# Relu of q on ScalarE from the fifth pair on, indicator rows of head 1 copied by VectorE, loads of pair 0 on one queue, and a new order

## The chip, the cores and the metric

The kernel runs on one core of a Trainium2 chip. A core has five engines, each of which works through its own list of instructions in order: PE (TensorE, matmuls and transposes), DVE (VectorE), ACT (ScalarE), POOL (GpSimd) and SP (SyncE, which here only issues DMAs). They meet at semaphores. DMAs move data between HBM and the on-chip memory SBUF, spread over 16 DMA engines. PE writes its results to PSUM, from where DVE and ACT read them; POOL reads SBUF alone.

The metric is the device time of one execution in microseconds (us).

## The reference

Two parts follow one another. The first is an attention with selected chunks, for 4 batches of 8 heads, 768 positions and 64 dimensions per head:

```
k_min, k_max = min and max of k over each chunk of 32 keys          # 24 chunks
ub     = sum_d max(q*k_min, q*k_max)                                # a bound per query and chunk
ub     = where(chunk of query >= chunk, ub, -1e9)
top    = the 6 chunks with the largest ub
mask   = (chunk of key in top) and (query >= key)
attn   = softmax(where(mask, q k^T / 8, -1e9))
x      = attn v, heads side by side                                 # 4 x 768 x 512
```

The second is a gated MLP on x, per batch:

```
h      = gelu(x w_in);  u, v = the two halves of h                  # 1024 -> 512 + 512
v_s    = w_sg (normalised v * g_ln) + b_sg                          # mixes the 768 positions
out    = x + (u * v_s) w_out
```

## The kernel before

*Pairs and windows.* The 32 heads are worked in 16 pairs (two heads share the 128 partitions). Buffers of a pair are reused: four windows (w = p % 4) of keys KA, queries QA and values vx, three sets of loaded rows (qn, kn, vn), three of transposed queries qT and of their relu rT.

*What happens to a pair* (`prep`, L1003). `kside` (L539): two DMAs bring the heads' rows of k; PE transposes them (L534), DVE takes minimum and maximum of each chunk of 32 (L562) into W, ACT evacuates the transposed k into KA (L439); DVE subtracts, so that W holds the minimum and the difference (L581). `qside` (L584): the same transposes for q, evacuated to qT by ACT (or by DVE for two pairs); then relu of columns 192 to 767 of qT into rT, a VectorE tensor_scalar with max 0 (L600); then POOL casts qT to bf16 into QA (L606). The bound is q times the minimum plus relu(q) times the difference, so the small matmuls `ub` (L641 for single pairs 0 to 3, L688 for pairs taken in twos from 4 on) need qT, rT and W of all their pairs. DVE transposes the bounds (L651, L697), finds the sixth largest of each row (`max`, L658, L708), compares (L664, L713) and transposes the result to Dt (L668, L716): one where a chunk isn't selected. Only columns from 192 on take part, since the first 192 queries have at most six chunks.

*How the mask reaches the scores.* For pairs 0 to 3 (`scores`, L772) extra matmuls (L804) add an indicator of the chunks times Dt to q k^T. From pair 4 on (`scores_full`, L736) each head has a window of its own, KA[w][0] and KA[w][1] of 128 rows: 64 rows of keys and 64 of the indicator INDF; the queries' window QA has Dt in the matching rows, brought by four DMAs from Dt on SP for each two pairs (L721). One matmul of 128 rows then gives the masked score (L757). ACT takes the exponential (L763, L813), POOL zeroes the part above the diagonal (L768, L820), PE multiplies by v (L836, L843), DVE divides (L851, L853).

*The indicator rows.* `mask_rows` (L725) runs when a window goes over from the first kind to the second, for windows 0 to 3. For both heads i it copies the 64 rows of INDF into KA[w][i], by a DMA on SP (L730), and has POOL clear the rows of QA (L733). For i = 0 the copy overwrites rows 64 to 127 of KA[w][0], in which the keys of the second head stood until then: it has to wait for the scores of pair w, and ACT's evacuation of k for pair w + 4 waits for it. Pairs 8 to 15 have their rows restored by another DMA (L578), after a DMA from KA to KA (L575).

*Loads.* Each load of q, k or v is one DMA per head on SP (L517, L526); for pair 0 alone the second head's loads of k and q go out from ACT's queue (`BOTH = 1`, used in L517). The weights follow on SP too.

*The MLP* (`moe_h` L871, `moe_g` L930) starts for each batch when its four pairs are done: transposes of x (L865, evacuated by ACT at L439), v half (L881, gelu L886), statistics (L891, L893) and normalising (L909) on DVE, u half (L920, gelu L926), the mixing (L938) with two DVE instructions per product (L955, L959), the last product (L971) and the residual (L980), then the store (L987).

*What sets the order.* The program is first written down as 1338 operations in the natural order (`P.op`, each with its engine, reads and writes). `TABLE` (L1057) then gives, for each engine, the order in which it issues them by their numbers, the PSUM slot of each tile and the places of some filler matmuls that keep PE busy at the start (L374). `Program.place` and `link` (L100, L122) take dependencies from the reads and writes, whatever the order, and turn them into semaphore waits. An engine waits at the head of its list: what is behind a waiting instruction waits too. That holds for the DMAs on SP as well.

Of the kernel before, what the change touches and what calls it, by code (L numbers as in the profile page):

```python
# [260 lines left out]
def _build(nc, ctx, q, k, v, w_in, g_ln, w_sg, b_sg, w_out, out):  # L261
    B, H, S, DH = q.shape
# [50 lines left out]
    BOTH = 1  # L313
    KBIG = 16
    VHACT = ()
    RELP = ()
    DNP = ()
# [266 lines left out]
    def qside(p):  # L584
# [14 lines left out]
        for x, (a, z) in enumerate(((LO, TG), (TG, S)) if p < RELH else ((LO, S),)):  # L599
            P.op("pool" if p in RELP else "dve", lambda d, a=a, z=z: d.tensor_scalar(  # L600
                rT[r][:, a - LO:z - LO], qT[r][:, a:z], 0.0, None, op0=ALU.max),
                gps(z - a, 60) if p in RELP else dve(z - a, rate=2), ("rel", p), port=True,
                reads=[qk[x]] if p < RELH else qk, writes=[("rT", r, x)] if p < RELH else [("rT", r, 0), ("rT", r, 1)])
# [121 lines left out]
    def mask_rows(w):  # L725

        for i in range(2):
            m0 = 64 * (1 - i)
            if i == 1 or (w if w >= HALF else w + NW) < KSPR:
                P.op("sp", lambda e, i=i, m0=m0: e.dma_start(KA[w][i][m0:m0 + 64, :], INDF[m0:m0 + 64, :]),  # L730
                     dmac(590), ("mrow", w, i, 0), reads=["INDF"], dma=f"mrow{i}", xfer=450,
                     writes=[("KI", w, i)] + ([("KA", w, 0, 0), ("KA", w, 0, 1)] if i == 0 else []))
# [303 lines left out]
    for p in range(4, NP + 4):  # L1036
# [39 lines left out]
    "act": (  # L1076
# [11 lines left out]
    "dve": (  # L1088
# [18 lines left out]
    "pool": (  # L1107
# [81 lines left out]
```

## Time and profile before

| | us |
|---|---|
| median of 3 runs | 221.12 (220.24 to 221.32) |
| the profiled execution | 221.28 |
| its span, from the first to the last instruction | 219.2 |
| PE busy in the span | 206.2 (94%) |
| DVE busy | 188.5 (86%) |
| ACT busy | 161.4 (74%) |
| POOL busy | 89.2 (41%) |

The profile names each group by line, engine, operation, and out<-in by the program's names, then the count, the busy time, the mean duration in ns, and the idle time of the engine just before, with what ended it. PEld is the loading of weights into PE, which overlaps PE's matmuls. Ends of matmuls are modelled, so PE busy is not PE at its peak. In lists of waits, "A <- B: total, times, longest" means that A's engine stood idle until B was done. SPq and ACTq are the engines' sequencers issuing DMAs. The chain of waits is followed back from the last instruction: at each step to what released it or to the instruction before it on its engine.

### The profile page before, as it was taken

To read this page: it belongs to the slowest core of one execution; us is meant where nothing else is said; L and a number is where in the kernel's file an instruction comes from. 1 tells how busy PE (TensorE), PEld (TensorE's weight loads), DVE (VectorE), ACT (ScalarE), POOL (GpSimd) and SP (SyncE) were. 2 spreads that over 40 slices of the span, in tenths; PEclk is the share of its full clock that TensorE was granted. 3 is DMA by queue.
4 is the path that set the end of the run, shared out by engine and by line. 5 is a ranking of instruction groups with operands and counts; after the bars stand their busy time and mean duration, and the time that the engine had idled before them with its cause. 6 is when DMAs were issued, how large, how long until landed. Compare 5 with 4: busy or idle time off the path is not lost.

```text
span 219.2 us, 6022 instructions
## 1 busy us (share of the span) xinstructions
PE 206.2 (94%) x2365; PEld 137.0 (63%) x2380; DVE 188.5 (86%) x542; ACT 161.4 (74%) x246; POOL 89.2 (41%) x119
## 2 busy tenths in 40 slices
PE   7969999899998999898999999999999999999994
PEld 3545768755756577686466676788745668545652
DVE  2899997879998999795999999998798776779894
ACT  3358989987469876799869787899986988764000
POOL 8415767973319445661323543663402141002000
PEclk9999999999999999999999999999999999999999
DMA  8999998993799998999999909433001002102107
GB/s 156 218 218 236 234 233 188 356 327 68 176 221 250 232 256 233 212 226 219 221 212 201 210 3 222 139 109 105 21 18 27 3 0 99 51 0 96 48 28 262
DMA packets 84651, 34.70 MB, mean 158 GB/s; under 512 B 77200, under 2 KB 79760, under 8 KB 84624
## 3 DMA queue, kind: packets, MB, share of 16 engines
q1 hardware_dynamic: 82768, 33.54, 63.8%
q10 hardware_dynamic: 1856, 0.79, 1.5%
q8 instruction: 19, 0.31, 0.7%
q14 instruction: 8, 0.07, 0.1%
HBM read 24.77 MB, written 6.29 MB: 142 GB/s over the span
## 4 chain that ended last, share of the span: by engine, by line
PE 61%; DVE 23%; ACT 7%; DMA 3%; SPq 3%; issue 2%; DVEq 0%; ACTq 0%
PE PSG L938 10%; PE PSC L757 9%; PE PSG L971 8%; PE PSG L534 6%; PE PSG L836 6%; PE PSG L920 5%; PE PSG L881 5%; DVE W L562 4%; ACT E L763 4%; DMA KA<-INDF 3%; PE PSG L688 3%; PE PSC L374 2%; PE PSG L843 2%; DVE stats L891 2%; PE PSC L798 2%; DVE PSG L955 2%
## 5 line engine op out<-in xcount | busy, mean ns | idle before, releaser
L763 ACT ACTIVATE E<-PSC 128x1024 bf16<-128x1024 f32 (+1 forms) x72 | 63.1, 924 | 6.4 <-PE PSC L757 5.8
L757 PE MATMUL PSC<-QA,KA 128*128 128x128 bf16 (+2 forms) x336 | 37.9, 246 | 1.1 <-ACT E L763 1.1
L562 DVE TENSOR_REDUCE W<-PSG 128x12 f32<-128x384 f32 x64 | 32.5, 545 | 4.5 <-PE PSG L534 4.4
L938 PE MATMUL PSG<-wsgT,vhat 128*128 128x384 bf16 x192 | 34.9, 326 | 0.8 <-DVE uT L959 0.4
L606 POOL CAST QA<-qT 64x768 bf16<-64x768 f32 (+1 forms) x28 | 24.2, 867 | 22.5 <-ACT qT L439 18.5
L768 POOL TENSOR_SCALAR_AFFINE_SELECT E<-E 128x768 bf16<-128x768 bf16 x24 | 20.8, 865 | 30.8 <-ACT E L763 30.4
L757 PEld LDWEIGHTS PSC<-QA,KA 128*128 128x128 bf16 x336 | 24.3, 98 | 10.3 <-ACT E L763 3.0
L926 ACT ACTIVATE uT<-PSG 128x384 bf16<-128x384 f32 x32 | 15.4, 492 | 16.6 <-PE PSG L920 16.0
L439 ACT ACTIVATE KA<-PSG 128x384 bf16<-128x384 f32 (+1 forms) x38 | 18.5, 493 | 10.1 <-DVE W L562 8.0
L938 PEld LDWEIGHTS PSG<-wsgT,vhat 128*128 128x128 bf16 x192 | 18.0, 98 | 12.1 <-DVE uT L959 0.9
L920 PE MATMUL PSG<-xT,winb 128*128 128x384 bf16 x128 | 24.1, 326 | 0.0
L813 ACT ACTIVATE E<-PSC 128x1024 bf16<-128x1024 f32 (+3 forms) x26 | 21.3, 858 | 3.6 <-PE PSC L804 3.4
L955 DVE SCALAR_TENSOR_TENSOR PSG<-PSG,glnT,bsgbc 128x384 f32<-128x384 f32 x32 | 19.7, 619 | 4.0 <-PE PSG L938 3.9
L881 PE MATMUL PSG<-winb,xT 128*128 128x512 bf16 x93 | 21.9, 379 | 0.2
L971 PE MATMUL PSG<-woutb,uT 128*128 128x512 bf16 (+1 forms) x88 | 21.1, 369 | 0.5
L836 PE MATMUL PSG<-vx,E 128*128 128x65 bf16 x480 | 19.6, 194 | 1.1 <-DVE XS L853 0.8
L836 PEld LDWEIGHTS PSG<-vx,E 128*128 128x128 bf16 x480 | 17.3, 98 | 2.8 <-DVE XS L853 1.1
L616 POOL CAST vx<-vn 128x768 bf16<-128x768 f32 x16 | 13.2, 828 | 13.7 <-DMA vn<-in_v_dram 7.7
L853 DVE TENSOR_TENSOR XS<-PSG,rden 128x384 bf16<-128x384 f32 x32 | 17.6, 554 | 0.8
L959 DVE TENSOR_TENSOR uT<-PSG,uT 128x384 bf16<-128x384 f32 x32 | 17.6, 554 | 0.8
L920 PEld LDWEIGHTS PSG<-xT,winb 128*128 128x128 bf16 x128 | 11.7, 98 | 9.8 <-ACT uT L926 1.4
L534 PE MATMUL PSG<-identF,kn 128*128 128x128 f32 x96 | 16.3, 288 | 1.4 <-ACT KA L439 0.8
(85 smaller groups left out, 345.6 us busy)
## 6 DMA issues: line engine op xcount, KB each, us to landing
vn<-in_v_dram SPq DMA_DIRECT2D x32, 192.0 KB, 4.1
kn<-in_k_dram SPq DMA_DIRECT2D x31, 192.0 KB, 4.5
qn<-in_q_dram SPq DMA_DIRECT2D x31, 192.0 KB, 4.5
out_dram<-osb SPq DMA_DIRECT2D x18, 256.0 KB, 2.8
uT<-in_moe_w_sg_dram SPq DMA_DIRECT2D x4, 384.0 KB, 6.5
KA<-INDF SPq DMA_DIRECT2D x16, 96.0 KB, 3.6
vgb<-in_moe_w_in_dram SPq DMA_DIRECT2D x3, 512.0 KB, 7.7
out_dram<-vgb SPq DMA_DIRECT2D x4, 256.0 KB, 2.0
```

The lines of the kernel that those rows point to most:

```text
L534: r = e.matmul(t.ap()[:, 128 * j:128 * j + 128], src[:, 3 * hf + j].rearrange("p i d -> p (i d)"), identF[:], is_transpose=True)
L562: P.op("dve", lambda d, m=m, op=op, src=src, h0=h0, h1=h1: d.tensor_reduce(W[w][:, m, 12 * h0:12 * h1].rearrange("p (h c) -> p h c", h=h1 ...
L606: P.op("pool", lambda g, i=i, r0=r0, r1=r1: g.tensor_copy(QA[w][i or 0][r0:r1, :], qT[r][r0:r1, :]), gps(S, 250 if i == 1 else 150), ("qca ...
L757: r = e.matmul(t.ap()[:, o:o + n], KA[w][i][:, 128 * kb:128 * kb + 128], QA[w][i][:, q0:q0 + n], start=True, stop=True)
L763: P.op("act", lambda e, t=t, c0=c0, c1=c1, i=i: e.activation(E[es][:, i, c0:c1], t.ap()[:, 0:c1 - c0], ACTF.Exp, scale=SCALE), act(c1 - c0 ...
L813: P.op("act", lambda e, t=t, c0=c0, c1=c1, n=n: e.activation(E[es][:, :, c0:c1], t.ap().rearrange("p (i x) -> p i x", i=2)[:, :, 0:n], ACT ...
L836: r = e.matmul(t.ap()[:, 65 * qb:65 * qb + 65], E[es][:, i, a:a + 128], vx[w][:, kb, i, :], start=first, stop=False, skip_group_check=True)
L881: r = e.matmul(t.ap()[:, 0:F], xT[s][:, dk, 128 * qt:128 * qt + 128], winb[:, dk, F:DFF], start=(dk == 0), stop=(dk == NDK - 1), skip_grou ...
L920: r = e.matmul(t.ap()[:, 0:TG], winb[:, dk, 128 * fb:128 * fb + 128], xT[s][:, dk, TG * tg:TG * tg + TG], start=(dk == 0), stop=(dk == NDK ...
L938: r = e.matmul(t.ap()[:, 0:TG], vhat[s][:, sb, 128 * fb:128 * fb + 128], wsgT[:, sb, TG * tg:TG * tg + TG], start=(sb == 0), stop=(sb == N ...
L955: P.op("dve", lambda d, t=t, fb=fb, tg=tg: d.scalar_tensor_tensor(t.ap()[:, 0:TG], t.ap()[:, 0:TG], glnT[:, fb:fb + 1], bsgbc[:, TG * tg:T ...
L971: r = e.matmul(t.ap()[:, 0:n1 - n0], gT[s][:, fb, 128 * qt:128 * qt + 128], woutb[:, fb, n0:n1], start=(fb == 0), stop=(fb == NF - 1))
```

## The change

- `BOTH` goes from 1 to 0: the two loads of pair 0 that ACT issued (k and q of its second head) are issued by SP. The four loads of pair 0 open its list: k of head 0, k of head 1, q of head 0, q of head 1.
- `RELA` is new and names pairs 4 to 15: their relu is an ACTIVATE with function Relu on ACT, over the same 576 columns from qT to rT, in place of DVE's tensor_scalar. Pairs 0 to 3 stay on DVE.
- `MRV` is new: in `mask_rows` the indicator rows for i = 0, of windows 0 to 3, are a DVE tensor_copy of 64 partitions by 768 bf16 from INDF, in place of a DMA on SP. For i = 1 the DMA stays.
- `TABLE` is new for all engines: the same operations by number, but with the twelve relus on ACT's list and off DVE's, the four copies on DVE's list and off SP's, and the two loads on SP's list and off ACT's. Many other operations change places by up to some 30 positions in their engine's list. The slots of the PSUM tiles change too; the fillers do not.

Places in the new lists that matter around the change: on ACT the relu of pair 4 stands behind the last exponential of pair 1, that of pair 5 behind the evacuation of xT for batch 0, those of 6 and 7 between evacuations of k and exponentials of pairs 4 and 5, those of 8, 10 and 9 ahead of the first exponential of pair 6, that of 11 ahead of the second batch's gelus, those of 12, 13 and 14 among the exponentials of pairs 8 and 9, that of 15 behind those of pair 11's second head. On DVE the copy for window 0 stands between the transposition and the maxima of pair 2's bounds, those for windows 1 and 2 around the last output of pair 1, that for window 3 behind the last output of pair 3 and ahead of pair 4's bounds. On SP the loads of k for pairs 6 and 7 go ahead of the first transfers of Dt (pairs 4 and 5), behind which they stood.

```diff
-    BOTH = 1
+    BOTH = 0
...
+    RELA = tuple(range(4,NP))
+    MRV = 1
...
         qk = [("qT", r, 0), ("qT", r, 1)]
-        for x, (a, z) in enumerate(((LO, TG), (TG, S)) if p < RELH else ((LO, S),)):
+        if p in RELA:
+            P.op("act", lambda e: e.activation(rT[r][:], qT[r][:, LO:S], ACTF.Relu), act(NSEL), ("rel", p), reads=qk,
+                 writes=[("rT", r, 0), ("rT", r, 1)])
+        for x, (a, z) in enumerate(((LO, TG), (TG, S)) if p < RELH else () if p in RELA else ((LO, S),)):
             P.op("pool" if p in RELP else "dve", lambda d, a=a, z=z: d.tensor_scalar(
...
         for i in range(2):
             m0 = 64 * (1 - i)
-            if i == 1 or (w if w >= HALF else w + NW) < KSPR:
+            if i == 0 and MRV and (w if w >= HALF else w + NW) < KSPR:
+                P.op("dve", lambda d: d.tensor_copy(KA[w][0][64:128, :], INDF[64:128, :]), (345, 430), ("mrow", w, 0, 0),
+                     port=True, reads=["INDF"], writes=[("KI", w, 0), ("KA", w, 0, 0), ("KA", w, 0, 1)])
+            elif i == 1 or (w if w >= HALF else w + NW) < KSPR:
                 P.op("sp", lambda e, i=i, m0=m0: e.dma_start(KA[w][i][m0:m0 + 64, :], INDF[m0:m0 + 64, :]),
...
 TABLE = {
...
     "sp": (
-        "29 31 33 34 35 40 36 39 68 41 37 42 69 38 66 67 132 128 127 126 129 44 178 43 136 213 180 179 75 177 "
...
+        "29 30 31 32 34 33 36 35 40 39 66 69 42 41 68 37 67 38 128 132 129 127 126 43 75 136 44 179 70 180 74 "
...
```

More of the change, by code (lines that the diff above doesn't have):

```diff
@@ L1058 @@
     "pe": (
[17 rows of a table removed]
-    "act": (
[11 rows of a table removed]
-    "dve": (
[18 rows of a table removed]
-    "pool": (
[14 rows of a table removed]
[17 rows of a table added]
+    "act": (
[11 rows of a table added]
+    "dve": (
[18 rows of a table added]
+    "pool": (
[14 rows of a table added]
     "slots": (
-        "1023312010323021100111013101000113302100011101023131123011100022110111000113210100101223000132233332"
-        "2222233233231110112300010101000321111011011010320001000101123010110133222323233322233223332323221011"
-        "0032010100011113210011001001003211011100101321010100233232322332232223233323323210110032010101023110"
-        "100023010110123102301113320210100303132210213"),
+        "1023301211322010101113010301001112312200000110123133023101001022101101101003201011001123303220322033"
+        "2332223223221110013200100011110321110011101011230010001010032010110132332233232223323223323333331000"
+        "1122101001011102210001000110102201010110010320111100232332322332322233322332232201001032101010133010"
+        "101132101010032013102330111002302323010211320"),
     "filler": (
```

116 rows, old and new, of the table TABLE are left out of this document.

## The prediction

> **What bounds the kernel now.** I read the stages first (busy time of each engine in ten stretches of the span; the stretches are cut where the busiest engine changes), then the chain of waits, then single groups. The first two lines are the page's busy times and the chain's shares; the columns of the stages are start:end, length, busy us of PE, PEld, DVE, ACT, POOL with instruction counts, granted clock, DMA share, GB/s.
>
> ```profile
> PE 206.2 (94%) x2365; PEld 137.0 (63%) x2380; DVE 188.5 (86%) x542; ACT 161.4 (74%) x246; POOL 89.2 (41%) x119
> ...
> PE 61%; DVE 23%; ACT 7%; DMA 3%; SPq 3%; issue 2%; DVEq 0%; ACTq 0%
> ```
>
> ```profile
> 0.00:28.00 28.00, 24.34 (x294) 15.21 (x295) 23.23 (x79) 16.89 (x28) 15.77 (x33) 1.00 1.12 212
> 28.00:46.00 18.00, 16.79 (x351) 12.62 (x349) 14.44 (x43) 17.25 (x27) 14.81 (x18) 1.00 1.00 273
> 46.00:66.00 20.00, 18.95 (x144) 11.63 (x137) 19.07 (x56) 13.41 (x24) 6.63 (x9) 1.00 0.73 179
> 66.00:88.00 22.00, 20.83 (x213) 14.63 (x216) 20.97 (x61) 17.76 (x29) 12.88 (x17) 1.00 1.02 243
> 88.00:103.00 15.00, 13.44 (x248) 10.99 (x250) 11.29 (x45) 13.55 (x20) 6.76 (x9) 1.00 0.99 221
> 103.00:130.00 27.00, 26.52 (x224) 16.86 (x224) 26.10 (x71) 22.05 (x35) 11.63 (x13) 1.00 0.80 180
> 130.00:141.00 11.00, 10.81 (x151) 7.53 (x150) 10.36 (x34) 8.90 (x13) 4.57 (x7) 1.00 0.66 166
> 141.00:158.00 17.00, 16.84 (x288) 13.45 (x289) 14.38 (x42) 16.90 (x25) 9.17 (x11) 1.00 0.28 86
> ```
>
> PE is the first bound: it is idle for 13.0 of 219.2 us, of which 3.7 lie before 28 and 5.8 between 28 and 158 by these rows, so the change can recover some 6 us in the middle at the very most. The granted clock is 1.00 in all these rows, so no term below is a clock term. Beside PE a second engine is full in each stage: ACT in 28 to 46 (0.75 us idle) and 141 to 158 (0.10 idle), DVE in 46 to 88 and 103 to 130 (about 1 us idle of each 20, 22 and 27). The relus leave DVE, which helps in DVE's stages, and land on ACT, which hurts in ACT's.
>
> The chain of waits, in order of time, through the two places where that is seen best:
>
> ```profile
> 44.97 1.28 PE PSG L688 x32
> ...
> 51.39 0.68 DVE Dt L716
> ...
> 59.02 6.37 DMA KA<-INDF
> 65.47 0.48 ACT KA L439
> ...
> 103.32 0.46 DVE rT L600
> ...
> 122.23 1.04 DVE rT L600
> ...
> 125.52 0.95 DVE rT L600
> ```
>
> From 103 to 128 the chain never leaves DVE, and three relus (L600) stand in it with 2.45 us. Before 65 it runs through the SP queue and one of the indicator transfers that the change replaces. Most of the chain's 61% of PE lies after 130.
>
> **The change part by part.** Durations come from the profiled execution, which took 221.28 us around its span of 219.2; that is 0.16 above the median of the runs, 221.12, and I take 0.16 off at the end.
>
> ```profile
> L600 DVE TENSOR_SCALAR rT<-qT 128x576 f32<-128x576 f32 x16 | 8.7, 549 | 2.7 <-ACT qT L439 2.7
> L439 ACT ACTIVATE qT<-PSG 128x384 f32<-128x384 f32 x28 | 13.4, 493 | 2.2 <-PE PSG L534 2.1
> L439 ACT ACTIVATE xT<-PSG 128x768 bf16<-128x768 bf16 x16 | 13.1, 825 | 2.3 <-PE PSG L865 2.2
> L401 DVE COPY IND<-IND 32x768 bf16<-32x768 bf16 x3 | 1.1, 352 | 0.1
> L763 ACT ACT_TABLE_LOAD x3 | 3.8, 1283 | 0.1
> ```
>
> And the relus by stage (busy us of DVE, count, clock, DMA share, GB/s), and what one takes (ns, least, median, most):
>
> ```profile
> 28.00:46.00 18.00, 1.10 (x2) 1.00 1.00 273
> 46.00:66.00 20.00, 0.44 (x1) 1.00 0.73 179
> 66.00:88.00 22.00, 0.90 (x2) 1.00 1.02 243
> 88.00:103.00 15.00, 0.90 (x2) 1.00 0.99 221
> 103.00:130.00 27.00, 2.62 (x3) 1.00 0.80 180
> 130.00:141.00 11.00, 0.46 (x1) 1.00 0.66 166
> 141.00:158.00 17.00, 0.61 (x1) 1.00 0.28 86
> ```
>
> ```profile
> L600 DVE TENSOR_SCALAR rT<-qT x16: 432/450/1125, 8.8 to 147.8; 128x576 f32<-128x576 f32 x16
> L730 SPq DMA_DIRECT2D KA<-INDF x8: 467/494/823, 25.5 to 79.7; - x8
> ```
>
> *Prices.* Twelve relus leave DVE: the four of the first stage stay, and the twelve of pairs 4 to 15 are 7.0 of the 8.7 us. The trace has no ACT relu. Nearest are the ACT evacuations of 384 and 768 columns, 493 and 825 ns; on the line between them 576 columns take 0.66 us. Ends: 0.45 (the median on DVE) and 0.83 (the 768-column row). I take 0.66, so ACT gets 7.9 us. Four copies of 64x768 come onto DVE, with the free size of L401's 0.35; the port end is the relus' own spread, 450 to 1125 ns, a factor 2.5, so 0.35 to 0.9 each; I take 0.4. Each indicator transfer leaves SP with 0.49 us of issue, four with 2.0; the two loads of pair 0 bring back about 1.0, by the SP rows of the start:
>
> ```profile
> 0.80 0.44 SPq L517 DMA_DIRECT2D kn<-in_k_dram  x1
> 0.80 0.49 ACTq L517 DMA_DIRECT2D kn<-in_k_dram  x1
> 1.24 3.59 PE L374 MATMUL PSC<-warm 128*128 128x512 bf16 x8 [1.24 <-DVE warm L371]
> ```
>
> The Trainium skill (ScalarE: Activation LUTs, What ACT_TABLE_LOAD costs) gives an ACTIVATE with immediate operands 186 ns plus 0.833 a column and lets neighbours overlap by 93; by that a relu would be 0.67, or 0.57 in a full queue, and the two stages of ACT below would come out 0.3 us cheaper in the sum. No run here has shown it for this form.
>
> *Start (pair 0's loads).* The first transposes need both heads of k. Head 1 is now issued 0.5 us later, behind head 0. The fillers (L374) keep PE until 4.83 in any case, so this costs between 0 and 1.0 (both added issues in full): I take +0.3. The loads behind them on SP go out up to 1.0 later until the first indicator transfer is left out, and 1.0 earlier after the fourth; ahead of the transfers PE's columns show no room that such a load left, so nothing for that.
>
> *Indicator copies.* Pair 0's copy stands between the transposes and the maxima of pair 2's selection, in a stage where DVE has no room after its first 5 us: +0.4 (0 to 0.9). Pairs 1 and 2 follow in 28 to 46, where DVE has 3.6 us idle, and pair 3's stands just ahead of the wait for pair 4's bounds, so these cost nothing; without that cover they cost 0.4 each.
>
> *28 to 46: relus of pairs 4 and 5.* ACT has 0.75 us idle here and gets 1.3. The bounds of pairs 4 and 5 (L688 at 44.97) need both, and in the new order relu 5 stands on ACT behind an xT evacuation. Behind the ACT queue wait the exponentials of pairs 2 and 3, and behind the bounds DVE's selection, Dt and the SP queue. DVE's 1.1 us of relu are no gain, since it waits there anyway. Between 0 and 1.3; nearer the full price since the queue is full: +1.0.
>
> *46 to 66: the indicator transfer.* These are the waits that go:
>
> ```profile
> ACT KA L439 <- DMA KA<-INDF: 1.7, 1, 1.7
> ```
>
> ```profile
> 61.83 1.74 PEld L938 LDWEIGHTS PSG<-wsgT,vhat 128*128 128x128 bf16 x12 [0.57 <-DVE vhat L909]
> ...
> 62.07 1.01 DVE L562 TENSOR_REDUCE W<-PSG 128x12 f32<-128x384 f32 x2
> ...
> 66.50 0.31 PEld L534 LDWEIGHTS PSG<-identF,kn 128*128 128x128 f32 x3 [1.19 <-ACT KA L439]
> ```
>
> ```profile
> qn<-in_q_dram SPq DMA_DIRECT2D x31, 192.0 KB, 4.5
> ```
>
> ACT waited 1.7 us for the rows of pair 2's window, PE 1.19 behind it. The DVE copy stands right behind pair 1's outputs in the new order, long before, and takes this away. What is late next is the k reduction itself, which ended at 63.08, 2.4 us before ACT's evacuation. One relu (0.44) leaves DVE here too. On SP the loads of k for pairs 6 and 7 now go ahead of the wait for Dt, but both loads of q for pair 6 stand behind it: Dt ended at 52.1, about seven issues of 0.5 and the 4.5 to landing make 60.1, and with Dt later by the +1.0 above 61.1. PE transposes this q, in the new order, just ahead of the mixing products that began at 61.83, so 0.7 of room. Between -2.1 and +1.0; I take PE's 1.2 and the 0.4, less 0.4 for those loads: -1.2.
>
> *66 to 103: relus 7 to 10.* DVE loses 1.8 us, of which the first half lies in a stage where it is full, but PE is idle only 1.2 us there; ACT gets 2.6 and has 4.2 + 1.5 idle. I take -0.5 for the former and +0.3 for the relus that stand just ahead of pair 6's exponentials, -0.2 in sum (-1.2 to +1.3).
>
> *103 to 130: relus 11 to 13.* They are the 2.45 us in the chain, and ACT has 5 us idle. PE's own work is next behind DVE (0.5 us idle by the stage's row, though PE busy counts modelled ends). Between 0 and -2.5; the chain is wholly DVE here, so I take most of it: -2.1.
>
> *130 to 215: relus 14 and 15.* ACT is full from 141 to 158, and the gelus of the third batch stand behind that queue. One of the two falls there: +0.6 (0 to 1.3). DVE's 1.1 us count nothing beside PE.
>
> Sum: 0.3 + 0.4 + 1.0 - 1.2 - 0.2 - 2.1 + 0.6 = -1.2. From 221.28 that is 220.1, on the scale of the runs 219.9. The ends add up to -5.8 and +6.8, but not together. The new order moves PE's pieces by up to 20 places; no row prices that, and I allow it the size of the largest single PE waits, 1.2 us either way.
>
> **The rivals.** *Nothing measurable.* PE holds. For it: PE is 94% busy by the page and the chain is 61% PE. Against: DVE's stages, where PE's fuller figure includes modelled ends. Then the gain of 103 to 130 falls to its 0.5 us of PE idle and the sum to +0.4: 221.5.
>
> *Slower: ACT becomes the bound.* Its place is the in-order ACT queue: each relu waits for both halves of q and makes the exponentials behind it wait. If around 28 to 46, 88 to 103 and 141 to 158 six relus (4, 5, 8, 9, 10, 15) come on the path with 0.66 each, that is 4.0 in place of the 1.9 that I put there (1.0, 0.3, 0.6), so 2.1 more; and the later bounds of pair 4 push all of DVE's full stretch behind them and cost the 1.2 of 46 to 66. The sum is then -1.2 + 2.1 + 1.2 = +2.1, and the time 223.2. It decides from about five relus on the path: 3.3 with the 0.7 of the start and the copy uses up the gains of 1.2, 0.5 and 2.1. For it: ACT's 0.75 and 0.10 idle. Against: ACT's 4.2 us idle in 66 to 88. The Trainium skill (ScalarE: Activation LUTs, Rules for kernel authors) says of relu to use VectorE and not ScalarE, for its higher rate; this trace agrees in the prices, 0.45 against the 0.66 worked out, but not on which engine has room.
>
> *The change doesn't do what it says.* Should a relu need another table than exp or gelu, twelve loads of 1.28 at the least come to 15.4 us: some 235. Exp needed three loads in all, though L439's copies run between its calls, so plain functions cost none here: 1 in 100.
>
> **How the numbers follow.** Change can be told from none beyond about 0.5%, 1.1 us. Faster, as summed: 0.42, with 218.0 to 220.0 as its own range and 219.9 as its time. Within: 0.29, at 221.5. Slower: 0.28 for ACT's queue at 223.2, and 0.01 for the tables. The range reaches from 217.8, near the sum with its three best terms at their ends (219.9 less 0.4, 0.9 and 1.0), to the slow rival's time of 223.2, and leaves out some 0.2, most of it half of that rival.
>
> **What would show it.** Right: no wait of ACT on KA<-INDF; the stretch from the first to the last product of the second batch on DVE shorter by about 2 us; DVE about 183 to 185 busy and ACT about 168 to 169; still eight table loads. Wrong: the bounds of pair 4 starting over 1.5 us later than 44.97 and DVE idle before them; exponentials of 28 to 46 or 141 to 158 drawn out; new PE waits on ACT over 1 us, above all in the new order's places.

## The result, and the profile after

The changed kernel takes 218.07 us in the median of its runs (217.51 to 218.63), against 220.68 us for the kernel before in the runs beside them (220.0 to 221.32). The ratio is 0.988, with a 95% interval of 0.984 to 0.993: 1.2% faster, 2.6 us. A second set of runs on another occasion gave 218.12 against 221.59, ratio 0.988 (0.983 to 0.993). Forecast were 219.9 us in a range of 217.8 to 223.2, and "faster" as the likeliest case. The ratios here and below are estimated from the executions within 1.5% of the fastest of their kernel, so they need not be the quotient of the medians.

The profiled execution took 217.9 us, with a span of 216.2. Its page, busy time by engine and the chain that ended last:

```profile
PE 206.0 (95%) x2380; PEld 136.2 (63%) x2380; DVE 184.8 (85%) x534; ACT 167.8 (78%) x258; POOL 88.8 (41%) x119
...
PE 75%; DVE 15%; ACT 5%; DMA 2%; issue 1%; SPq 0%; DVEq 0%
```

PE is about as busy as before (206.0 against 206.2 us), so what was gained is PE's idle time in the main. DVE gave up 3.7 us of busy time and ACT took 6.4. The chain is now PE for 75% of the span instead of 61%, and DVE's part of it fell from 23% to 15%. By stages (the columns are those of the same table in the prediction):

```profile
0.00:28.00 28.00, 25.48 (x322) 15.79 (x324) 23.52 (x84) 18.80 (x32) 16.21 (x34) 1.00 1.11 213
28.00:46.00 18.00, 15.60 (x332) 11.54 (x329) 15.58 (x41) 16.32 (x26) 15.25 (x18) 1.00 1.04 288
46.00:66.00 20.00, 19.45 (x140) 11.98 (x138) 18.34 (x58) 15.89 (x27) 7.91 (x11) 1.00 0.84 199
66.00:88.00 22.00, 22.00 (x257) 15.44 (x263) 21.52 (x63) 20.13 (x34) 12.95 (x16) 1.00 0.97 212
88.00:103.00 15.00, 13.84 (x223) 10.56 (x208) 11.22 (x42) 14.54 (x22) 6.65 (x8) 1.00 0.89 225
103.00:130.00 27.00, 26.73 (x235) 17.58 (x234) 25.15 (x72) 22.89 (x39) 9.51 (x11) 1.00 0.91 177
130.00:141.00 11.00, 11.00 (x168) 8.08 (x166) 9.83 (x38) 10.53 (x16) 5.90 (x8) 1.00 0.51 147
141.00:158.00 17.00, 17.00 (x272) 12.91 (x270) 13.62 (x48) 16.97 (x24) 7.45 (x9) 1.00 0.27 81
```

PE's idle time in a stage is the stage less PE's busy time; the last row of the table is what is left of the whole (219.2 less 206.2, and 216.2 less 206.0). Set beside the same rows of before, and beside the prediction's terms, it tells where the time went:

| stage (us) | PE idle before | after | change | predicted |
|---|---|---|---|---|
| 0 to 28 | 3.7 | 2.5 | -1.1 | +0.7 |
| 28 to 46 | 1.2 | 2.4 | +1.2 | +1.0 |
| 46 to 66 | 1.0 | 0.6 | -0.5 | -1.2 |
| 66 to 103 | 2.7 | 1.2 | -1.6 | -0.2 |
| 103 to 130 | 0.5 | 0.3 | -0.2 | -2.1 |
| 130 to the end | 3.9 | 3.3 | -0.6 | +0.6 |

The idle time falls by 2.8 us in all. Some of that is no gain: the profile of before lacks 15 of the 2380 matmul records (x2365 on its page), and where they are missing 14 gaps of about 53 ns count as idle, 0.74 us together, 0.47 of them in the last row. The changed kernel's profile lacks none, so the -0.6 of the last row is mostly these records, and the other rows move by 0.16 at most. The sum of the forecast has the right sign and about half the size, but nearly every row differs: the 2.1 us of 103 to 130 weren't there to be had, and 66 to 103, put at nearly nothing, gave most. The runs below were made to find out why.

The new instructions themselves, least, median and most in ns; the table loads, which are eight as before; and the copies' mean:

```profile
L602 ACT ACTIVATE rT<-qT x12: 674/682/757, 26.7 to 140.9; 128x576 f32<-128x576 f32 x12
...
L735 DVE COPY KA<-INDF x4: 357/536/1193, 24.5 to 44.2; 64x768 bf16<-64x768 bf16 x4
...
L894 ACT ACT_TABLE_LOAD x4 | 5.1, 1283 | 0.1
L771 ACT ACT_TABLE_LOAD x3 | 3.8, 1283 | 0.1
L735 DVE COPY KA<-INDF 64x768 bf16<-64x768 bf16 x4 | 2.6, 656 | 0.1
...
L422 ACT ACT_TABLE_LOAD x1 | 1.3, 1283 | 0.8 <-PEq L1182 0.8
```

A relu on ACT takes 0.68 us, predicted 0.66. A copy takes 0.36 to 1.19 us, 0.66 in the mean, predicted 0.4 within 0.35 to 0.9.

### The profile page after: what moved, and what is told of

Same layout as the page of the kernel before. It is cut to its first block, busy times and chain, and to the rows that moved or that the text cites. A ratio compares the mean times of both kernels' runs of the same rounds, so it can differ in the third digit from the quotient of the medians.

```text
span 216.2 us, 6033 instructions
## 1 busy us (share of the span) xinstructions
PE 206.0 (95%) x2380; PEld 136.2 (63%) x2380; DVE 184.8 (85%) x534; ACT 167.8 (78%) x258; POOL 88.8 (41%) x119
## 4 chain that ended last, share of the span: by engine, by line
PE 75%; DVE 15%; ACT 5%; DMA 2%; issue 1%; SPq 0%; DVEq 0%
PE PSG L946 15%; PE PSC L765 11%; PE PSG L979 10%; PE PSG L928 9%; PE PSG L889 8%; PE PSG L536 7%; PE PSG L844 6%; DVE W L564 5%; PE PSG L693 3%; ACT E L771 3%; PE PSG L851 2%; DVE stats L899 2%; DMA kn<-in_k_dram 2%; PE PSG L873 1%; PE PSC L806 1%
## 5 line engine op out<-in xcount | busy, mean ns | idle before, releaser
L564 DVE TENSOR_REDUCE W<-PSG 128x12 f32<-128x384 f32 x64 | 32.7, 547 | 7.0 <-PE PSG L536 6.9
L963 DVE SCALAR_TENSOR_TENSOR PSG<-PSG,glnT,bsgbc 128x384 f32<-128x384 f32 x32 | 19.6, 619 | 5.1 <-PE PSG L946 4.9
L979 PE MATMUL PSG<-woutb,uT 128*128 128x512 bf16 (+1 forms) x100 | 23.7, 371 | 0.0
L821 ACT ACTIVATE E<-PSC 128x1024 bf16<-128x1024 f32 (+3 forms) x26 | 21.5, 872 | 2.2 <-PE PSC L812 1.8
L889 PE MATMUL PSG<-winb,xT 128*128 128x512 bf16 x96 | 22.7, 380 | 0.2 <-ACT xT L441 0.2
L967 DVE TENSOR_TENSOR uT<-PSG,uT 128x384 bf16<-128x384 f32 x32 | 17.6, 554 | 0.7
L905 POOL TENSOR_TENSOR rstd<-rstd,neghalf 128x6 f32<-128x6 f32 x4 | 5.3, 1329 | 31.2 <-DVE rstd L903 31.2
L899 DVE BATCH_NORM_STATS2 stats<-vgb 128x6 f32<-128x512 f32 x24 | 16.1, 687 | 2.0 <-ACT vgb L894 1.6
```

Of the source, the lines that this page charges most:

```text
L564: P.op("dve", lambda d, m=m, op=op, src=src, h0=h0, h1=h1: d.tensor_reduce(W[w][:, m, 12 * h0:12 * h1].rearrange("p (h c) -> p h c", h=h1 ...
L821: P.op("act", lambda e, t=t, c0=c0, c1=c1, n=n: e.activation(E[es][:, :, c0:c1], t.ap().rearrange("p (i x) -> p i x", i=2)[:, :, 0:n], ACT ...
L889: r = e.matmul(t.ap()[:, 0:F], xT[s][:, dk, 128 * qt:128 * qt + 128], winb[:, dk, F:DFF], start=(dk == 0), stop=(dk == NDK - 1), skip_grou ...
L899: P.op("dve", lambda d, qt=qt, st=st: d.bn_stats(stats[st][:], vg[qt]), dve(F, 60), ("bns", b, qt), reads=[("vg", qt)], writes=[("stats", ...
L979: r = e.matmul(t.ap()[:, 0:n1 - n0], gT[s][:, fb, 128 * qt:128 * qt + 128], woutb[:, fb, n0:n1], start=(fb == 0), stop=(fb == NF - 1))
```

## The experiments

Two theories stood against each other. *Parts*: the gain is the sum of what each moved instruction is worth where it stands, as the prediction summed it. *Fit*: the moved instructions and the new order are worth something only together, since the order decides which engine is full where the instructions land. All ratios are to the kernel before, run beside them; microseconds are 1% = 2.2.

**The moved instructions on the old order.** First only the twelve relus, each put into ACT's order at the time at which DVE had started it; then the copies and the loads of pair 0 as well.

```diff
 # b_rela: all tables as in the kernel before, but
+    RELA = (4, 5, 6, 7, 8, 9, 10, 11, 12, 13, 14, 15)
 # "act": ... kev 4, exp 2, [rel 4], exp 2, qev 5 ... exp 3, [rel 5], kev 5 ...
 # b_all: the same, and
-    BOTH = 1
+    BOTH = 0
+    MRV = (0, 1, 2, 3)
```

> The order of before with the twelve relus alone on ACT. By the prediction's terms for the relus (+1.0, -0.4, -0.2, -2.1, +0.6) 1.1 faster than before, about 219.6, with most of it in 103 to 130. If ACT is held up instead: 221 to 222.5. If the relus don't matter: 220.7.

> The order of before with all three moves put into it (twelve relus on ACT where DVE began them, four copies on DVE behind the scores that free the rows, four loads of pair 0 on SP). If the moves make the gain: 218.0 to 219.2. If the new order makes it: 220.2 to 222, since ACT then has 7 us more in a list that was not arranged for it.

Measured: the relus alone 1.008 (1.005 to 1.011), all the moves 1.007 (1.004 to 1.010). Both are slower than before, by 1.8 and 1.6 us, where the prediction's terms had the relus alone 1.1 faster. The page of the kernel with the relus alone, its chain by engine, and from the chain in order of time the pieces that are relus (start, us, what):

```profile
PE 54%; ACT 23%; DVE 13%; DMA 5%; SPq 3%; issue 1%; DVEq 0%; ACTq 0%
```

```profile
33.59 0.57 ACT rT L602
...
42.36 0.56 ACT rT L602
...
74.91 0.57 ACT rT L602
...
102.46 0.57 ACT rT L602
...
105.44 0.69 ACT rT L602
...
106.13 1.28 ACT L894
...
141.60 0.68 ACT rT L602
...
150.37 0.56 ACT rT L602
```

Seven of the twelve relus (pairs 4, 5, 7, 10, 11, 14 and 15) stand on the chain, with 4.2 us together, one of them (pair 11) right ahead of a table load of 1.28. ACT's share of the chain went from 7% to 23%. This is the prediction's rival "ACT becomes the bound", with its size and nearly its point (it was to decide from about five relus on the path): on the old order it is what happens. In the changed kernel's first profile no relu on ACT is on the chain; in its second one is, that of pair 5 with 0.58 us (from 42.95, ahead of the bounds of pair 4). The pieces of 0.57 beside a duration of 0.68 also agree with the estimates that the prediction worked out from the Trainium skill (ScalarE: Activation LUTs, What ACT_TABLE_LOAD costs), 0.67 alone and 0.57 in a full queue.

**The new order with the moves taken back.** First all of them, then only the relus (copies and loads stay as in the changed kernel); each relu goes into DVE's order at the time at which ACT had started it. "New order" stands for all of the new `TABLE`, the PSUM slots with it; they were not tried apart.

```diff
 # a_order: the new order, and
-    BOTH = 0
+    BOTH = 1
-    RELA = tuple(range(4,NP))
+    RELA = ()
-    MRV = 1
+    MRV = ()
 # a_norela: the new order, and only RELA = ()
```

> The order of after with all three moves undone (relus on DVE where ACT began them, indicator transfers on SP where DVE began the copies, two loads of pair 0 on ACT). If the moves make the gain: 220 to 221. If the new order makes it: 217.8 to 219.

> The order of after with the twelve relus back on DVE, copies and loads as in after. If the relus carry the gain: 219.2 to 220.5. If the order carries it: 217.8 to 218.5. If the relus on ACT cost, as the prediction's terms for 28 to 46 and 141 to 158 have it, without a gain on DVE: below 217.8.

Measured: the order alone 1.010 (1.007 to 1.014), with copies and loads 1.006 (1.004 to 1.009). Both are slower than any time expected for them: that the new order without the relus on ACT would be a loss was not foreseen. The order alone costs 2.3 us and the moves alone 1.6, and together they gain 2.6. They don't add up; *Parts* falls. In the new order the twelve relus on ACT are worth 1.0062 less 0.9883, 1.8% or 4.0 us (about 1.3 either way by the two intervals), where on the old order the same move costs 1.8.

The same instructions' start times in the profiles show where (us; the bounds are L641 for pair 2 and L688 from pair 4 on, L646 and L693 by the lines of the changed kernel; the last column is the last matmul of the output, L971 or L979). From pair 4 on, all these orders have nearly the same number of matmuls ahead of the bounds on PE, within 3%:

| kernel | bounds of pair 2 | pair 4 | pair 8 | pair 12 | pair 14 | last output matmul |
|---|---|---|---|---|---|---|
| before | 24.9 | 45.0 | 91.1 | 135.5 | 155.7 | 215.7 |
| relus alone, old order | 24.6 | 45.6 | 92.7 | 137.3 | 158.0 | 218.0 |
| new order alone | 23.1 | 45.0 | 92.2 | 137.6 | 157.5 | 217.6 |
| changed, relus on DVE | 23.0 | 45.0 | 91.6 | 137.2 | 157.2 | 217.2 |
| changed | 22.6 | 44.2 | 87.5 | 132.7 | 152.7 | 212.7 |
| changed, second profile | 23.0 | 43.7 | 86.7 | 132.1 | 152.1 | 212.2 |

Up to pair 4 the changed kernel and the one with relus on DVE differ by 0.8 us, at pair 8 by 4.1, and from pair 12 on by about 4.5. The gain is made between 46 and 91. Against the kernel before, the changed kernel leads by 0.8 us at pair 4 and by 3.6 at pair 8, and ends 3.0 ahead. The loss from pair 2 to pair 4 (its lead falls from 2.2 to 0.8 us, in the second profile from 1.8 to 1.3) is there with the relus on DVE too, so it is the order's and not the relus'.

**Which relus?** From the changed kernel, five relus go back to DVE, or three others; the changed kernel itself ran again for comparison (ratio 0.988, the second set above).

```diff
 # a_d6_10
-    RELA = tuple(range(4,NP))
+    RELA = (4, 5, 11, 12, 13, 14, 15)
 # a_d11_13
+    RELA = (4, 5, 6, 7, 8, 9, 10, 14, 15)
```

> The changed kernel itself again, beside the next three on one chip. In the runs so far the moves alone on the old order (1.007 of the time before), and the order alone (1.010), are both slower than before. Theory 'fit' (the relus on ACT pay only in places that the new order gives them, and the new order pays only with DVE relieved): 0.986 to 0.991 of the time before again, that is 218.4 to 219.5 where before takes 221.5. Rival 'chip' (the gain of the changed kernel belonged to the chip it was taken on): 0.997 to 1.005.

> The changed kernel with the relus of pairs 6 to 10 back on DVE. Theory 'DVE sets 60 to 91' (the new order needs DVE free of these five): with all twelve relus back, the profile fell from 0.7 us behind the changed kernel at the bounds of pair 4 to 4.1 behind at those of pair 8, so five relus alone cost 2.3 to 3.3 us here and nothing after 91: 220.6 to 221.6 where the changed kernel takes 218.1. Rival (the prediction's step for 66 to 103): 0.2 to 0.5 us, 218.3 to 218.6.

> The changed kernel with the relus of pairs 11 to 13 back on DVE. The prediction's step for 103 to 130: they cost 2.1 us, 220.2 where the changed kernel takes 218.1. Rival 'PE is next' (with all twelve back on DVE the stage lost only 0.5 us, and with these relus on ACT the chain of waits of 110 to 130 is PE's own work): 0.3 to 0.8 us, 218.4 to 218.9.

Measured: with relus 6 to 10 on DVE 1.001 (0.998 to 1.005), which is 2.9 us over the changed kernel's 0.988 (1.3 either way): all of the gain is gone. With relus 11 to 13 on DVE 0.992 (0.988 to 0.997), 0.9 us over it, but 1.5 either way: the runs alone don't tell that from nothing.

The row of 66 to 88 and the chain of 66 to 92 by line, of the kernel with relus 6 to 10 on DVE:

```profile
66.00:88.00 22.00, 20.82 (x195) 13.67 (x192) 21.50 (x60) 15.48 (x27) 11.55 (x15) 1.00 0.90 196
```

```profile
by line: DVE W L564 19.6%; DVE PSG L963 12.5%; DVE uT L967 11.4%; DVE osb L988 9.9%; DVE rT L605 8.6%; DVE U L702 5.5%; DVE m L713 5.3%; DVE Dn L718 5.1%; PE PSG L693 3.4%; issue 3.2%; DVE Dt L721 2.6%; PE PSG L844 2.4%; DVE XS L861 2.1%; P
```

the same two of the changed kernel's second profile:

```profile
66.00:88.00 22.00, 21.89 (x268) 15.35 (x269) 21.00 (x62) 20.24 (x32) 12.91 (x16) 1.00 1.03 220
```

```profile
by line: PE PSC L765 20.4%; PE PSG L979 19.5%; PE PSG L536 16.2%; ACT E L771 14.3%; PE PSG L946 13.2%; PE PSG L693 8.7%; PE PSG L844 5.3%; ACT xT L441 2.7%; PE PSG L851 2.1%; issue 0.5%
```

and the chain of the same stretch in the kernel before, whose row for 66 to 88 stands in the prediction:

```profile
by line: PE PSG L938 18.8%; PE PSC L757 18.2%; PE PSG L534 15.7%; PE PSG L971 12.9%; PE PSG L688 7.6%; ACT E L763 7.1%; PE PSG L836 5.4%; ACT KA L439 5.3%; DVE W L562 3.6%; DVE osb L980 2.7%; PE PSG L843 2.1%; issue 1.0%
```

These rows are the core of the case. DVE is full in all three (21.5, 21.0 and 21.0 of 22 us). In the new order with the relus on it, the chain runs through DVE from line to line, k's reductions (L564), the gates (L963, L967), the outputs' additions (L988) and the relus themselves at 8.6%. From 62 to 88 all five relus stand in it, with 2.75 us together, which is nearly the 2.9 that the runs lost. PE is busy for 20.8 us of the stage. Without these relus the chain is PE and some ACT, and PE is busy for 21.9. (The counts, 195 and 268 products, mix long and short ones and aren't the same work.) In the old order the chain of this stretch was PE's and not DVE's although the relus were on DVE: it is the new order that makes DVE the bound there.

Why the new order with the relus on DVE is slower than the old one is not shown by this. The kernel with all relus on DVE ends 1.5 us behind the kernel before; it is 0.5 behind at the bounds of pair 8 and 1.7 at those of pair 12, so most of that arises behind this stretch.

For relus 11 to 13, the chain of 115 to 130 in the kernel that has them on DVE, first by line and then the pieces that are relus and the first product behind them:

```profile
by line: PE PSG L946 19.6%; DVE PSG L963 14.3%; DVE uT L967 14.3%; PE PSC L765 12.5%; PE PSG L536 8.9%; DVE rT L605 6.5%; DVE vhat L917 6.1%; PE PSG L979 5.8%; DVE Dn L718 5.0%; DVE Dt L721 4.6%; DVE m L713 4.4%; issue 0.9%
...
118.14 0.37 DVE rT L605
...
121.96 0.60 DVE rT L605
...
123.08 1.15 PE PSG L946 x6
```

and of the changed kernel:

```profile
by line: PE PSG L946 49.8%; PE PSC L765 27.1%; PE PSG L536 14.0%; PE PSG L979 5.8%; PE PSG L844 3.0%; PE PSG L851 1.2%
```

Two relus with 1.0 us were on a chain of DVE; with them gone the chain is PE's alone, from end to end. By start times, the kernel with these relus on DVE is 1.85 us behind the changed kernel's second profile at the second group of mixing products of batch 1 (116.53 against 114.68), most of it from before 74 us, where the two run the same instructions; at the outputs of pair 8 it is 2.38 behind (129.92 against 127.54). The stage itself costs it 0.5. So by the profiles 0.5 to 1.0 us is what these relus hold, not 2.1; the runs alone would leave both open.

**The copies.** The changed kernel with the four indicator rows by transfers again, in two sets of runs.

```diff
 # a_nomrv, a_nomrv2: the new order, relus on ACT, and
-    MRV = 1
+    MRV = ()
 # the four numbers of the copies go from "dve" to "sp", by start time
```

> The changed kernel with the four indicator rows of head 1 by the SP queue's transfers again, in the places of the copies. Theory 'the indicator wait' (prediction's step for 46 to 66): the copies are worth 0.8 us (1.2 less 0.4), so 219.3 where before takes 221.5, with a wait of ACT on the indicator transfer of 1 us or more. Rival 'DVE's time': the new order has room around the transfer, and DVE gets the 2.6 us of the copies back, 0.2 to 0.8 less than the changed kernel: 217.9 to 218.4.

> The kernel with the indicator rows of head 1 by transfers again, a second time: its first profile shows ACT waiting 3.0 us for a transfer that took up to 7.8 us to land, and its twelve times spread from 218.05 to 222.74. Theory 'late landing': the median is 0.5 to 1.6 us over the changed kernel's, 218.6 to 219.7, with a spread of over 3 us and a wait of ACT on the indicator transfer of 0.5 to 3 us in the profile. Rival 'no wait': within 0.4 of 218.1, no such wait.

Measured: 0.991 (0.988 to 0.995) and 0.993 (0.990 to 0.997), so 0.7 and 1.1 us over the changed kernel, each with about 1.4 either way. Both agree with the 0.8 that the prediction's two terms give (1.2 for the wait less 0.4 for a copy), though neither resolves it well. In the pair of kernels of the new order without ACT relus, the copies and loads together were worth 0.4%, 0.9 us, but no wait for the transfer shows in that profile (`a_order`), so this says nothing on the wait. The first profile is of the longest of its twelve executions (222.74 us) and is left out here. The second has the wait, and a stage row with a lower granted clock:

```profile
ACT KA L441 <- DMA KA<-INDF: 1.4, 1, 1.4
```

```profile
28.00:46.00 18.00, 15.63 (x317) 12.26 (x324) 12.35 (x36) 15.46 (x24) 15.47 (x19) 0.91 0.97 260
```

ACT waits 1.4 us for the rows, but in this order already between 28 and 46, where DVE is busy 3.2 us less than in the changed kernel's row above. The granted clock of the stage is 0.91; it is 1.00 in the changed kernel, where no such wait is. The trace shows where it fell. PE stands idle for 2.17 us, from 39.56 to 41.73; in steps of 2 us the clock is 1.00 up to 42, then 0.50 from 42 to 44, 0.64 from 44 to 46, and 1.00 again. ACT had the rows only at 40.88, and the exponential behind them ended at 41.63, just before PE went on. In the changed kernel PE's pause at this place is 0.59 us (40.59 to 41.18). So a part of what the copies save here is the clock, and the prediction had no clock term.

**The start, and more relus.** The changed kernel with head 1 of pair 0's loads issued by ACT again; with the relus of pairs 0 to 3 on ACT too; and with both.

```diff
 # a_noboth
-    BOTH = 0
+    BOTH = 1
 # a_rel16
-    RELA = tuple(range(4,NP))
+    RELA = tuple(range(NP))
 # a_best: both
```

> The changed kernel with one head of pair 0's loads issued by ACT again. Theory (prediction's step for the start): 0.3 us less than the changed kernel, 218.3 where before takes 221.5, with the first transposes of k about 0.25 earlier. Rival: the q of pair 0 comes later on ACT's queue (7.19 against 6.50 us in the two profiles), and the time is 0.3 to 0.7 longer: 218.9 to 219.3.

> The changed kernel with the relus of pairs 0 to 3 on ACT too. They take 0.46, 0.44, 0.45 and 1.12 us of DVE, which is busy 18.71 of 19 us from 9 to 28. Theory 'DVE sets 9 to 30': ACT has 1 to 2 us idle at pairs 0 and 1 (8.9 to 10.8, 12.9 to 14.0) and PE waits 1.2 us for the relu of pair 3, so 0.8 to 2.0 us less than the changed kernel: 216.5 to 217.9 where before takes 221.5. Rival 'ACT sets 14 to 46': the relus of pairs 2 and 3 hold up the exponentials by 0.5 to 0.7 each and the gain is eaten: 218.2 to 219.5.

> The changed kernel with all sixteen relus on ACT and one head of pair 0's loads issued by ACT again. Alone these gave 0.9874 and 0.9865 against the changed kernel's 0.9883 in one set of runs. If both are real they add to 0.4 to 0.6 us less than the changed kernel, 217.5 to 217.8; if they are noise, within 0.4 of 218.1.

Measured: 0.987 (0.982 to 0.991), 0.987 (0.983 to 0.991) and 0.985 (0.980 to 0.990), against 0.988 (0.983 to 0.993) for the changed kernel. None is told apart from it. The start's loads may cost the predicted 0.3 us, and the runs would not show it. The four relus of DVE's full first stage (18.7 of 19 us busy between 9 and 28 in the changed kernel) are worth less than the 0.8 to 2.0 expected: by their profile the bounds of pair 4 start at 44.2, where the changed kernel's two profiles have 44.2 and 43.7. What sets the pace of 28 to 46 in the new order was not found; PE, DVE and ACT each are idle there for 1.7 to 2.4 us of 18 in the changed kernel's first profile. The combination has the lowest ratio of all, but whether it is really faster stays open.

## Why the prediction was right or wrong

*Right in the sign, with less than half of the size, and that by luck in good part.* The forecast gain was 1.2 us, measured are 2.6, and 218.07 lies close to the lower end of the range, 217.8. The terms came out as follows.

*Prices.* The relu on ACT was right (0.66 for 0.68). DVE's and ACT's busy times, forecast at 183 to 185 and 168 to 169, came out at 184.8 and 167.8, and the table loads stayed at eight. The copy was mis-sized at 0.4 for 0.66 in the mean. The two long ones stand where the prediction named cover; the one for window 0 is on the chain with 0.36 (at 24.47), as its term of 0.4 had it.

*Start, +0.7 for loads and copy.* PE's idle time of 0 to 28 fell by 1.1 instead (by 0.8 in the second profile), and the bounds of pair 2 came 1.8 to 2.2 us earlier. The new order does it alone: with all moves taken back they start at 23.1, against 24.9 before. The loads' own +0.3 wasn't resolved.

*28 to 46, +1.0 for relus 4 and 5.* On the old order this is exactly what they do: both are on the chain with 0.57 and 0.56, and the bounds of pair 4 fall back by 0.9 us against those of pair 3 (30.7 to 30.5, then 45.0 to 45.6). In the new order the stage does lose 1.2 in the first profile, but it loses 1.6 with the relus on DVE, so that loss isn't the relus'. In the second profile it loses 0.2, although relu 5 is on the chain there. The number agreed by accident; the mechanism holds for the old order.

*46 to 66, -1.2 for the indicator wait.* The wait is gone. With what the copies cost taken off, its worth is 0.7 and 1.1 by the two sets of runs, where the terms give 0.8, but a part of that is the lower clock. In the new order with the relus on ACT it would have stood one stage earlier.

*66 to 103, -0.2 for relus 7 to 10.* This is the step that failed, together with the allowance of 1.2 us either way for the order. "PE is idle only 1.2 us there" was read from a stage of the old order, where the chain is PE's. In the new order relus 6 to 10 hold 2.9 us (relu 6, put at 0.4 in the stage before, among them), since that order makes DVE the chain of the whole stretch as long as they are on it.

*103 to 130, -2.1 for relus 11 to 13.* This step failed the other way. PE's work was directly behind DVE's, as the row with 0.5 us of PE idle said; the prediction set that row aside because PE's busy time counts modelled ends. The chain of the changed kernel is PE from 115 to 130, and the relus held 0.5 to 1.0 us. The rival "PE holds" had this stage right. The sign that the prediction set here, the products of the second batch shorter on DVE by about 2 us, came, and even double: from the first L955 to the last L959 it was 18.7 us, and it is 14.3 (L963 to L967). But it is 14.8 with relus 11 to 13, or all twelve, back on DVE, so nearly all of that is the order.

*130 to 215, +0.6 for relus 14 and 15.* On the old order both are on the chain (141.60 and 150.37) and the bounds of pair 14 fall back by 0.6 against those of pair 12. In the new order they aren't on it. From the bounds of pair 12 to the last output matmul it takes 80.0 us in both profiles of the changed kernel and 80.2 in the one before, so what is gained there is 0.2; the -0.6 of the table is mostly the missing records.

*The rival "ACT becomes the bound"* described the relus on the old order: seven on the chain, 1.8 us slower. What kept it from coming true is the new order. Relu 4 and relus 7 to 15 start 3.6 to 18 us earlier in the changed kernel than in the one before, in places where ACT isn't the last to arrive. Against the moves on the old order, the whole group begins at 26.7 in place of 33.5 and ends at 140.9 in place of 150.3:

```profile
L602 ACT ACTIVATE rT<-qT x12: 674/685/712, 33.5 to 150.3; 128x576 f32<-128x576 f32 x12
```

That is the row of the relus on the old order; the changed kernel's stands above. The durations are nearly the same in both (medians 685 and 682 ns), so the price of a relu isn't what differs. Which of the order's many moves matters was not tried apart.

## What to carry to other kernels

When instructions change engines and the order changes with them, the stages of the old profile price the moves only for the old order: walk the new order through its full engine stage by stage, and ask which engine is the chain there with and without the moved work. An engine that is busy for 21 of 22 us in both versions can be the bound in one and not in the other; the chain by line tells them apart, the busy share doesn't. And where a second engine's row shows 0.5 us of idle time in a stage, a gain beyond that needs a reason of its own.

## What was not expected of the hardware

The 64x768 copies on DVE spread from 357 to 1193 ns within one execution, a factor of 3.3, wider than the relus' 432 to 1125 of before; in the second profile the longest took 0.72 us. A pause of PE of 2.17 us (in the kernel with the indicator rows by transfers) was followed by a granted clock of 0.50, while pauses of 1.59 us (13.68 to 15.27 in the kernel before) and 1.18 us (28.43 to 29.61 in the changed kernel) left it at 1.00; whether the length alone decides was not tried. And two profiles of the identical changed kernel differ by up to 0.8 us in the middle (bounds of pair 6 at 72.2 and 71.4 us) before they end 0.5 apart, so single profiles say nothing about terms below that.
